# Retention and ELU feed-forward in one kernel: earlier weight loads, two-bank turns and another order of the matrix work

## The chip, the cores and the metric

The kernel runs on one core of a Trainium2 chip. The metric is the device time of one execution in microseconds (us). Before the change it was 322.56 us, the median of three runs (321.85 to 322.69). Lower is better.

## The reference, cut to what matters

```python
# q, k, v: (8, 8, 576, 64) float32; w_in (512, 2048), w_out (2048, 512)
scores = (1 / sqrt(64)) * q @ k.transpose(0, 1, 3, 2)
gamma  = 1 - 2 ** (-5 - arange(8))
Dmat   = where(rel >= 0, gamma ** rel, 0)        # rel = query position - key position
attn   = (scores * Dmat) @ v
x      = attn.transpose(0, 2, 1, 3).reshape(4608, 512)
h      = x @ w_in                                # "FFN1"
g      = where(h > 0, h, exp(min(h, 0)) - 1)     # ELU
out    = g @ w_out                               # "FFN2"
```

The kernel cuts the 4608 rows into 36 units of 128 rows. A unit goes through these steps: load q, k, v; cast to bf16; turn q and k (a transpose); scores; mask; products with v and with a running state; x. FFN1 and FFN2 work on groups of one to four units. Units 0 to 11 are turned by TensorE, units 12 to 35 by a DMA transpose.

## The kernel before

These are the parts that the change and the argument touch. Cuts are marked with `...`. The pools `ps_s`, `ps_h`, `ps_o` and so on lie in PSUM, the memory that TensorE writes its results to; a tile is a named buffer in a pool. A bank is a part of PSUM. A slot is one piece of FFN1 or FFN2 work in the order that the kernel builds. V, A and G are copies on VectorE, ScalarE and GpSimd. The w_in weights come in four pieces, one for each call of `load_w_in`.

```python
def turn(u, bank=None):
    t = tpool.tile([P, 2, HP, P], BF16, ...)
    n = kns[u]
    if u < PE_TURNED:                                  # 12
        pool, tag = bank or (ps_s, "sc")
        ps = pool.tile([P, 2, HP, P], BF16, name="tr", tag=tag)      # one tile for both halves
        for c in range(2):
            for hp in range(HP):
                nc.tensor.transpose(ps[:, c, hp], n[:, c, hp * P : (hp + 1) * P], ident)
        nc.vector.tensor_copy(t[:, 0], ps[:, 0])
        nc.scalar.copy(t[:, 1], ps[:, 1])
    else:
        nc.sync.dma_start_transpose(...)
    qkTs[u] = t

def finish(n=0):                                       # the ELU's last step, some slots late
    while late and late[0][0] <= slot[0] - n:
        _, gt_, ph, m, _ = late.pop(0)
        nc.vector.scalar_tensor_tensor(gt_, ph, 0.0, m, ALU.max, ALU.min)

# the start: units 0 to 2, then FFN1 of group 0
for u in range(3):
    scores(u); inter(u); state(u); masks(u)
    if u == 1:
        G(seen, raws[2][0][0:1, 0, 0, 0:1])            # GpSimd waits for unit 2's q ...
        load_w_in(0)                                   # ... and only then issues w_in
    if u < 2:
        cast(u + 1, A, G); scale_v(u + 1); dummy(3); turn(u + 1, h)
    else:
        for n in range(1, 4): load_w_in(n)
        load_w_out(0, 0, 8); load_w_out(0, 8, 16)
        dummy(6)                                       # warm-up matmuls, result not used
    intra(u); put_x(u); state_out(u); dummy(2)
...
for n in range(16):
    f1(0, n, m if n % 4 == 3 else None)
    if n == 3: turn(3)
    if n == 5:
        scale_v(3)
        load_w_out(1, 0, 16)                           # issued by GpSimd in mid-FFN1
    if n == 7: scores(3); masks(3)                     # one 128x1024 instruction
    if n == 11: product(3)
...
# steady part: FFN1 slots of group g merged with FFN2 slots of group g-1
while a < len(f1s) or b < len(f2s):
    if b * len(f1s) < a * len(f2s) and b < len(f2s) or a >= len(f1s):
        slots.append(f2s[b]); b += 1
    else:
        slots.append(f1s[a]); a += 1
```

## Time and profile before

| what | value | where it is read |
|---|---|---|
| span of the profiled execution | 320.8 us | first line of the page |
| TensorE (PE) busy | 305.0 us, 95% | busy table |
| VectorE, ScalarE, GpSimd busy | 58%, 43%, 45% | busy table |
| first FFN1 matmul | 19.99 us | timeline of PE |
| first FFN2 matmul | 37.76 us | timeline of PE |
| wait for an ELU result | 1.50 us at 27.8 us | timeline of PE |
| PE idle, 56 to 72 us | 2.20 us | windows |

Three lines of the page follow: busy us and share of the span for each engine; the busy tenths of PE in 40 slices; and the share of the DMA engines.

```profile
PE 305.0 (95%) x2961; PEld 173.4 (54%) x2998; DVE 185.9 (58%) x295; ACT 137.3 (43%) x255; POOL 143.5 (45%) x224
...
PE   7878999899999999999999999999999999999995
...
DMA  9999999997999999999898969777225200000021
```

Nothing but PE is near its limit over the whole span, so only PE's idle time can be won. The DMA engines are busy for most of the first 200 us (6 to 9 tenths in each of the first 25 slices).

The timeline of PE at the start (start us, duration, engine, line, operation, output and inputs, count, and in brackets the idle time before it and what ended it; `ph` is FFN1's result, `tr` a turn, `sc` the scores):

```profile
19.99 2.77 PE L322 MATMUL ph<-xt,w_in_sb 128*128 128x384 bf16 x16 [1.48 <-DMA w_in_sb<-in_moe_w_in_dram]
22.60 0.61 PE L190 MATMUL tr<-ident,qkn 128*128 128x128 bf16 x8
23.31 2.77 PE L322 MATMUL ph<-xt,w_in_sb 128*128 128x384 bf16 x16
26.01 0.42 PE L206 MATMUL sc<-qkT 64*64 64x128 bf16 x16
26.36 1.47 PE L322 MATMUL ph<-xt,w_in_sb 128*128 128x384 bf16 x8
29.34 1.46 PE L322 MATMUL ph<-xt,w_in_sb 128*128 128x384 bf16 x8 [1.50 <-DVE g L306]
```

PE waits 1.48 us for the first piece of w_in and later 1.50 us for VectorE's ELU result. GpSimd's timeline shows what held that result:

```profile
25.93 1.04 POOL L177 TENSOR_TENSOR vn<-rv,gk 128x512 bf16<-128x512 f32 x1
26.92 1.22 POOL L100 DMA_DIRECT2D w_out_sb<-in_moe_w_out_dram  x1
28.17 1.94 POOL L329 TENSOR_SCALAR m<-e 128x384 bf16<-128x384 f32 x4
```

The four `m` steps of the ELU stand behind the 1.22 us issue of a weight load.

Later, around unit 6, the chain of waits shows PE with nothing to run (start us, duration, what):

```profile
58.61 0.44 DVE qkT L191
...
59.07 0.59 ACT qkT L192
...
59.71 0.45 PE sc L206 x16
...
60.18 1.23 DVE pt L215
61.40 0.61 DVE xt L279
...
62.05 1.00 PE ph L322 x15
```

The turn's two copies run one after the other, and then mask and x separate the scores from the next FFN1. Both kinds of PE waits (first the copies, then x) stand in PE's timeline as 0.24 us and 1.23 us:

```profile
59.71 0.42 PE L206 MATMUL sc<-qkT 64*64 64x128 bf16 x16 [0.24 <-ACT qkT L192]
...
62.05 1.05 PE L322 MATMUL ph<-xt,w_in_sb 128*128 128x128 bf16 x16 [1.23 <-DVE xt L279]
```

The next lines are from the table of waits of ScalarE and from the windows view (stretch; length; PE busy and matmuls; PEld busy and weight loads; DVE; ACT; POOL; granted clock; DMA share; GB/s; the granted clock is the share of full TensorE speed that the profile records):

```profile
ACT qkT L192 <- DVE qkT L191: 9.4, 10, 2.5
```

```profile
56.00:72.00 16.00, 13.80 (x282) 11.38 (x277) 11.24 (x16) 8.52 (x17) 10.50 (x15) 1.00 1.02 212
...
104.00:180.00 76.00, 74.54 (x737) 39.76 (x748) 53.76 (x83) 34.17 (x67) 38.25 (x59) 1.00 1.02 191
180.00:300.00 120.00, 119.26 (x923) 57.14 (x936) 68.22 (x95) 50.11 (x88) 47.97 (x72) 1.00 0.44 96
```

### The profile page before, as it was taken

The page shows a single profiled execution, that of the slowest core. Times are in us where ns is not written, and L with a number is a line of the kernel's source. Part 1 is how long each engine was busy: PE and PEld are TensorE (multiplying, and loading weights), DVE is VectorE, ACT ScalarE, POOL GpSimd, SP SyncE. Part 2 cuts the span into 40 slices and gives each one's busy share as a digit, 9 for nine tenths or more (in the row PEclk, how much of TensorE's full clock was granted, in tenths as well). Part 3 has the DMA queues.
Part 4 walks back from the last instruction along what each step waited for, and adds up shares of the span by engine and source line. Part 5 has one row for each costly group of instructions (what it writes and reads, how often), then busy time and mean ns, then how long its engine had stood idle before and what let it go on. Part 6 is the DMA issues. An engine that isn't in the chain of part 4 may idle for free.

```text
span 320.8 us, 7515 instructions
## 1 busy us (share of the span) xinstructions
PE 305.0 (95%) x2961; PEld 173.4 (54%) x2998; DVE 185.9 (58%) x295; ACT 137.3 (43%) x255; POOL 143.5 (45%) x224
## 2 busy tenths in 40 slices
PE   7878999899999999999999999999999999999995
PEld 3544888776766555555444444444444444444444
DVE  3656713766668677676676666666666655433400
ACT  6335513545543445444444444344444444434411
POOL 2867530755644555454444444444444433333300
PEclk9999999999999999999999999999999999999999
DMA  9999999997999999999898969777225200000021
GB/s 169 216 213 200 175 232 255 212 206 180 222 163 221 237 194 182 187 227 168 165 218 166 181 134 219 163 167 166 67 65 68 65 35 35 33 33 33 36 98 65
DMA packets 150195, 48.72 MB, mean 152 GB/s; under 512 B 138640, under 2 KB 146192, under 8 KB 150160
## 3 DMA queue, kind: packets, MB, share of 16 engines
q1 hardware_dynamic: 141888, 41.76, 65.4%
q0 software_dynamic: 6256, 4.19, 8.8%
q10 hardware_dynamic: 2016, 2.29, 2.6%
q8 instruction: 23, 0.38, 0.5%
q14 instruction: 12, 0.10, 0.1%
HBM read 36.70 MB, written 9.44 MB: 144 GB/s over the span
## 4 chain that ended last, share of the span: by engine, by line
PE 85%; DMA 4%; DVE 4%; issue 2%; SPq 2%; POOL 1%; ACT 1%; POOLq 0%
PE ph L322 37%; PE pm L347 32%; PE pmh L363 6%; PE sc L206 4%; DMA w_in_sb<-in_moe_w_in_dram 3%; PE o L266 2%; PE st L249 2%; PE o L232 2%; SPq L86 2%; DMA rqk<-in_q_dram 2%; DVE pt L215 1%; PE tr L190 1%; POOL m L329 1%; DVE xt L279 1%; ACT qkT L192 1%
## 5 line engine op out<-in xcount | busy, mean ns | idle before, releaser
L329 POOL TENSOR_SCALAR m<-e 128x512 bf16<-128x512 f32 (+1 forms) x156 | 92.2, 592 | 147.2 <-ACT e L327 139.8
L322 PE MATMUL ph<-xt,w_in_sb 128*128 128x512 bf16 (+3 forms) x820 | 144.9, 313 | 5.4 <-DVE g L306 1.7
L306 DVE SCALAR_TENSOR_TENSOR g<-ph,m 128x512 bf16<-128x512 f32 (+1 forms) x156 | 99.9, 647 | 81.7 <-POOL m L329 80.4
L327 ACT ACTIVATE e<-ph 128x512 f32<-128x512 f32 (+1 forms) x156 | 88.0, 564 | 123.0 <-PE ph L322 119.1
L347 PE MATMUL pm<-w_out_sb,g 128*128 128x512 bf16 x474 | 121.4, 379 | 2.3 <-issue 1.6
L322 PEld LDWEIGHTS <-w_in_sb 128*128 128x128 bf16 x832 | 71.9, 98 | 60.9 <-issue 3.6
L347 PEld LDWEIGHTS <-g 128*128 128x128 bf16 x496 | 47.2, 98 | 52.7 <-issue 0.5
L215 DVE TENSOR_TENSOR pt<-sc,mask 128x1024 bf16<-128x1024 f32 x36 | 44.0, 1222 | 14.4 <-PE sc L206 14.4
L177 POOL TENSOR_TENSOR vn<-rv,gk 128x512 bf16<-128x512 f32 x36 | 37.8, 1052 | 2.5 <-DMA rv<-in_v_dram 1.5
L279 DVE TENSOR_TENSOR xt<-o,gx 128x512 bf16<-128x512 f32 x36 | 24.5, 681 | 3.4 <-PE o L266 3.4
L354 ACT COPY ot<-pm 128x512 f32<-128x512 f32 x31 | 18.1, 585 | 16.7 <-PE pm L347 16.5
L258 ACT CAST sb<-st 128x256 bf16<-128x256 f32 x32 | 11.9, 373 | 18.1 <-PE st L249 15.3
L363 PE MATMUL pmh<-w_out_sb,g 128*128 128x256 bf16 x160 | 18.5, 273 | 0.5 <-ACT oth L375 0.5
L206 PEld LDWEIGHTS <-qkT 64*64 64x64 bf16 x576 | 9.2, 106 | 15.4 <-issue 9.1
L206 PE MATMUL sc<-qkT 64*64 64x128 bf16 x576 | 15.0, 222 | 2.2 <-ACT qkT L192 2.2
L363 PEld LDWEIGHTS <-g 128*128 128x128 bf16 x160 | 15.4, 98 | 2.8 <-issue 0.6
L168 DVE CAST qkn<-rqk 128x1024 bf16<-128x1024 f32 x24 | 16.4, 683 | 0.0
L266 PE MATMUL o<-pt,vn 128*64 128x128 bf16 x288 | 14.4, 221 | 0.0
L232 PE MATMUL o<-qkT,sb 64*64 64x128 bf16 (+1 forms) x256 | 12.3, 214 | 0.0
L384 PE MATMUL dum<-warm 128*128 128x512 bf16 x35 | 10.9, 431 | 1.4 <-DVE warm L108 1.3
L192 ACT COPY qkT<-tr 128x512 bf16<-128x512 bf16 x12 | 7.0, 583 | 9.5 <-DVE qkT L191 9.4
L249 PE MATMUL st<-vn,qkn 128*64 128x64 bf16 (+1 forms) x256 | 10.5, 200 | 0.6 <-POOL vn L177 0.6
(43 smaller groups left out, 82.0 us busy)
## 6 DMA issues: line engine op xcount, KB each, us to landing
rqk<-in_q_dram SPq DMA_DIRECT2D x32, 256.0 KB, 3.9
rqk<-in_k_dram SPq DMA_DIRECT2D x32, 256.0 KB, 4.3
rv<-in_v_dram SPq DMA_DIRECT2D x32, 256.0 KB, 4.6
out_dram<-ot SPq DMA_DIRECT2D x27, 256.0 KB, 2.3
w_in_sb<-in_moe_w_in_dram POOLq DMA_DIRECT2D x4, 512.0 KB, 9.5
out_dram<-oth ACTq DMA_DIRECT2D x9, 128.0 KB, 3.3
w_out_sb<-in_moe_w_out_dram POOLq DMA_DIRECT2D x2, 512.0 KB, 15.2
w_out_sb<-in_moe_w_out_dram POOLq DMA_DIRECT2D x1, 1024.0 KB, 12.7
```

The costliest lines, as they stand in the source:

```text
L177: nc.gpsimd.tensor_tensor(n, rv, gk[:, u % R].unsqueeze(2).to_broadcast([P, H, D]), ALU.mult)
L206: nc.tensor.matmul(sc[j * 64 : (j + 1) * 64, i, hp], t[r, 1, hp, j * 64 : (j + 1) * 64], t[r, 0, hp], start=(hp == 0), stop=(hp == HP - 1) ...
L215: nc.vector.tensor_tensor(pt.rearrange("p i h t -> p (i h) t"), scs[u].rearrange("p i h t -> p (i h) t"), m.unsqueeze(1).to_broadcast([P, ...
L232: nc.tensor.matmul(o[rows, hp, :n], sbs[u][rows, hp], qkTs[u][rows, 0, hp, :n], start=(hp == 0), stop=False, skip_group_check=True,)
L266: nc.tensor.matmul(o[i * D : (i + 1) * D, hp], vns[u][:, h], pts[u][:, i, hp], start=(u % R == 0 and hp == 0), stop=(hp == HP - 1), skip_g ...
L279: nc.vector.tensor_tensor(xts[g][:, :, i * P : (i + 1) * P], os_[u], gx[:, :, s0 : s0 + P], ALU.mult)
L306: nc.vector.scalar_tensor_tensor(gt_, ph, 0.0, m, ALU.max, ALU.min)
L322: nc.tensor.matmul(ph[:, i * n : (i + 1) * n], w_in_sb[:, j, f : f + P], xts[g][:, j, :n], start=(j == 0), stop=(j == KJ - 1), skip_group_ ...
L327: nc.scalar.activation(e[:, w], ph[:, w], AF.Exp)
L329: nc.gpsimd.tensor_scalar(m[:, w], e[:, w], -1.0, 1.0, ALU.add, ALU.mult)
L347: nc.tensor.matmul(pm, gts[g, ft][:, it * P : (it + 1) * P], w_out_sb[:, ft], start=(ft == 0), stop=(ft == NFT - 1))
L363: nc.tensor.matmul(pm, gts[g, ft][:, it * P : (it + 1) * P], w_out_sb[:, ft, c * 256 : c * 256 + 256], start=(ft == 0), stop=(ft == NFT - 1),)
```

## The change

Its intent is to take away waits of PE: bring w_in sooner; let VectorE and ScalarE copy a turn's halves at the same time from two banks; shorten what stands in front of ELU results; keep an FFN2 slot between a unit's scores and the FFN1 that needs its x; and shorten the end. The diff, cut to its core:

```diff
     def turn(u, bank=None):
-            ps = pool.tile([P, 2, HP, P], BF16, name="tr", tag=tag)
+            if bank:                                   # units 0 to 2
+                ps = [pool.tile([P, HP, P], BF16, name="tr", tag=tag) for c in range(2)]
+            else:                                      # units 3 to 11
+                both = ps_s.tile([P, 2, 2, HP, P], BF16, name="tr", tag="sc")
+                ps = [both[:, c, 0] for c in range(2)]
...
     def ffn2(g, s):
-        if late and (g, part * 4 + 3) >= late[0][4]:
-            finish()
+        while late and (g, part * 4 + 3) >= late[0][4]:
+            finish(slot[0] - late[0][0])               # no more than is needed
...
-        if u == 1:
-            G(seen, raws[2][0][0:1, 0, 0, 0:1])
-            load_w_in(0)
         if u < 2:
             cast(u + 1, A, G)
+            if u == 0:
+                load_w_in(0)
...
             load_w_out(0, 8, 16)
-            dummy(6)
+            load_w_out(1, 0, 16)
+            dummy(3)
...
             scale_v(3)
-            load_w_out(1, 0, 16)
         if n == 7:
             scores(3)
-            masks(3)
+            masks(3, 0)
+        if n == 8:
+            masks(3, 1)
+        if n == 9:                                     # before: after f1(1, 0)
+            load(4, nc.vector)
+            for u in range(5, 12): load(u)
...
-    ffn2_half(0, 1, m)
+    ffn2_half(0, 1, h)
     turn(4); ffn2_half(1, 1, h); scores(4); masks(4)
-    ffn2_half(2, 1, h); product(4); prep(5, A, G)
-    ffn2_half(3, 1, h); turn(5); f1(2, 0); scores(5); masks(5); prep(6, A, G)
-    f1(2, 1); f1(2, 2); turn(6); f1(2, 3)
+    prep(5, A, G); ffn2_half(2, 1, h); product(4)
+    turn(5); ffn2_half(3, 1, m); scores(5); masks(5); prep(6, A, G)
+    f1(2, 0); f1(2, 1); turn(6); f1(2, 2)              # f1(2, 3) becomes the first slot
...
-            if b * len(f1s) < a * len(f2s) and b < len(f2s) or a >= len(f1s):
+            if b * len(f1s) <= a * len(f2s) and b < len(f2s) or a >= len(f1s):
...
-            due[u] = due[last] + (start[g] - 1.6 - due[last]) * (u - last) / (u1 - last)
+            due[u] = due[last] + (start[g] - 1.0 - due[last]) * (u - last) / (u1 - last)
+        if PE_TURNED <= u + 3 < NU:                    # DMA transposes
+            events.append((at(0.4) if u + 2 < PE_TURNED else due[u], -1, u + 3))
...
-    for c in range(2):
-        ffn2_half(NU - 1, c, ((ps_s, "sc"), h)[c])
+    ffn2_cols(u, 0, 256, (ps_s, "sc"), V, nc.scalar)
+    ffn2_cols(u, 256, 384, h, A, nc.scalar)
+    ffn2_cols(u, 384, 512, (ps_st, "st"), V, nc.sync)
```

More of the change, by code (lines that the diff above doesn't have):

```diff
@@ L185, in turn @@
         if u < PE_TURNED:
-            pool, tag = bank or (ps_s, "sc")
-            ps = pool.tile([P, 2, HP, P], BF16, name="tr", tag=tag)
+            if bank:
+                pool, tag = bank
+                ps = [pool.tile([P, HP, P], BF16, name="tr", tag=tag) for c in range(2)]
+            else:
+                both = ps_s.tile([P, 2, 2, HP, P], BF16, name="tr", tag="sc")
+                ps = [both[:, c, 0] for c in range(2)]
             for c in range(2):
                 for hp in range(HP):
-                    nc.tensor.transpose(ps[:, c, hp], n[:, c, hp * P : (hp + 1) * P], ident)
-            nc.vector.tensor_copy(t[:, 0], ps[:, 0])
-            nc.scalar.copy(t[:, 1], ps[:, 1])
+                    nc.tensor.transpose(ps[c][:, hp], n[:, c, hp * P : (hp + 1) * P], ident)
+            nc.vector.tensor_copy(t[:, 0], ps[0])
+            nc.scalar.copy(t[:, 1], ps[1])
         else:
@@ L210, in scores, with masks @@
         scs[u] = sc
-    def masks(u):
-        pt = ppool.tile([P, 2, HP, P], BF16, name="pt", tag="pt")
+    def masks(u, i=None):
+        if u not in pts:
+            pts[u] = ppool.tile([P, 2, HP, P], BF16, name="pt", tag="pt")
         m = mask[:, 1 if u % R == 4 else 0]
+        s = slice(0, 2) if i is None else slice(i, i + 1)
         nc.vector.tensor_tensor(
-            pt.rearrange("p i h t -> p (i h) t"), scs[u].rearrange("p i h t -> p (i h) t"),
-            m.unsqueeze(1).to_broadcast([P, 2 * HP, P]), ALU.mult,
+            pts[u][:, s].rearrange("p i h t -> p (i h) t"), scs[u][:, s].rearrange("p i h t -> p (i h) t"),
+            m.unsqueeze(1).to_broadcast([P, (s.stop - s.start) * HP, P]), ALU.mult,
         )
-        pts[u] = pt
     def inter(u):
@@ L355, in ffn2, with ffn2_cols, ffn2_half @@
             (nc.scalar if i0 < 8 * P else nc.sync).dma_start(out[i0 : i0 + P, :], ot)
-    def ffn2_half(u, c, bank):
+    def ffn2_cols(u, c0, c1, bank, copy, queue):
         g, it = group_of[u]
         pool, tag = bank
-        pm = pool.tile([P, 256], FP32, name="pmh", tag=tag)
+        pm = pool.tile([P, c1 - c0], FP32, name="pmh", tag=tag)
         for ft in range(NFT):
             nc.tensor.matmul(
-                pm, gts[g, ft][:, it * P : (it + 1) * P], w_out_sb[:, ft, c * 256 : c * 256 + 256],
+                pm, gts[g, ft][:, it * P : (it + 1) * P], w_out_sb[:, ft, c0:c1],
                 start=(ft == 0), stop=(ft == NFT - 1),
             )
-        ot = opool.tile([P, 256], FP32, name="oth", tag="ot")
-        rows = out[u * P : (u + 1) * P, c * 256 : c * 256 + 256]
-        if u == NU - 1 and c == 1:
-            nc.scalar.copy(ot[:, :128], pm[:, :128])
-            nc.scalar.dma_start(rows[:, :128], ot[:, :128])
-            nc.vector.tensor_copy(ot[:, 128:], pm[:, 128:])
-            nc.sync.dma_start(rows[:, 128:], ot[:, 128:])
-        else:
-            (nc.scalar.copy if u % 2 else nc.vector.tensor_copy)(ot, pm)
-            nc.scalar.dma_start(rows, ot)
+        ot = opool.tile([P, c1 - c0], FP32, name="oth", tag="ot")
+        copy(ot, pm)
+        queue.dma_start(out[u * P : (u + 1) * P, c0:c1], ot)
+    def ffn2_half(u, c, bank):
+        ffn2_cols(u, c * 256, c * 256 + 256, bank, A if u % 2 else V, nc.scalar)
     V, A, G = nc.vector.tensor_copy, nc.scalar.copy, nc.gpsimd.tensor_copy
@@ L390, in prep @@
             scale_v(u)
-            if u >= PE_TURNED:
-                turn(u)
     nload = [12]
@@ L408 @@
     h, m = (ps_h, "ph"), (ps_m, "pm")
-    seen = const.tile([1, 1], FP32, name="seen")
     dummy(18)
@@ L453 @@
             scale_v(3)
-            load_w_out(1, 0, 16)
         if n == 7:
             scores(3)
-            masks(3)
+            masks(3, 0)
[3 more added lines that the diff above has]
+            load(4, nc.vector)
+            for u in range(5, 12):
+                load(u)
         if n == 11:
@@ L461 @@
         f1(1, n, m if n == 3 else None)
-        if n == 0:
-            load(4, nc.vector)
-            for u in range(5, 12):
-                load(u)
     finish()
@@ L474 @@
     masks(4)
+    prep(5, A, G)
     ffn2_half(2, 1, h)
     product(4)
-    prep(5, A, G)
-    ffn2_half(3, 1, h)
     turn(5)
-    f1(2, 0)
+    ffn2_half(3, 1, m)
     scores(5)
@@ L483 @@
     prep(6, A, G)
+    f1(2, 0)
     f1(2, 1)
+    turn(6)
     f1(2, 2)
-    turn(6)
-    f1(2, 3)
-    slots, start, now = [], {}, 0.0
+    slots, start, now = [(f1, 2, 3, 1.0)], {}, 1.0
     for g in range(3, NG + 1):
+        f1s, f2s = [], [(ffn2, g - 1, s, 1.0) for s in range(4 * len(GROUPS[g - 1]))]
+        if g < NG:
+            per = 4 // len(GROUPS[g])
+            f1s = [(f1, g, s, per * len(GROUPS[g]) / 4) for s in range(NFT // per)]
+        else:
+            f2s = f2s[:-4]
+        a, b = 0, 2 if g == 4 else 0
+        slots += f2s[:b]
+        now += b
         start[g] = now
-        f1s = [(f1, g, s, k * len(GROUPS[g]) * P / 512) for k in [4 // len(GROUPS[g])] for s in range(NFT // k)] if g < NG else []
-        n2 = len(GROUPS[g - 1]) - (g == NG)
-        f2s = [(ffn2, g - 1, s, 1.0) for s in range(4 * n2)]
-        a = b = 0
         while a < len(f1s) or b < len(f2s):
-            if b * len(f1s) < a * len(f2s) and b < len(f2s) or a >= len(f1s):
+            if b * len(f1s) <= a * len(f2s) and b < len(f2s) or a >= len(f1s):
                 slots.append(f2s[b])
@@ L513, with at @@
     for u in range(5, NU):
+        def at(share):
+            return due[u] + share * (due[u + 1] - due[u])
         events.append((due[u], 0, u))
         if u + 2 < PE_TURNED:
-            events.append(((due[u] + due[u + 1]) / 2, 1, u + 2))
+            events += [(due[u], -1, u + 2), (at(0.5), 1, u + 2)]
+        if PE_TURNED <= u + 3 < NU:
+            events.append((at(0.4) if u + 2 < PE_TURNED else due[u], -1, u + 3))
     events.sort()
@@ L522 @@
             _, kind, u = events.pop(0)
-            if kind == 1:
-                turn(u)
-                continue
-            if u + 2 < PE_TURNED:
-                prep(u + 2, A, G)
-            if u + 3 >= PE_TURNED:
-                prep(u + 3, V)
-            load_next()
-            stretch(u)
+            if kind == -1:
+                prep(u, *((A, G) if u < PE_TURNED else (V,)))
+                if u >= PE_TURNED:
+                    turn(u)
+            elif kind == 1:
+                turn(u)
+            else:
+                load_next()
+                stretch(u)
         f(g, s)
         now += d
-    for c in range(2):
-        ffn2_half(NU - 1, c, ((ps_s, "sc"), h)[c])
+    u = NU - 1
+    ffn2_cols(u, 0, 256, (ps_s, "sc"), V, nc.scalar)
+    ffn2_cols(u, 256, 384, h, A, nc.scalar)
+    ffn2_cols(u, 384, 512, (ps_st, "st"), V, nc.sync)
 _INS = ['q', 'k', 'v', 'moe_w_in', 'moe_w_out']
```

## The prediction

> **What bounds the kernel.** TensorE: 305.0 us busy of a 320.8 us span (busy table), granted clock 1.00 in every slice. The change removes no matrix work but three warm-up matmuls, so it can only shorten TensorE's 15.8 us of idle. By the windows table that idle lies: about 3.2 us before 16 us, 1.5 in 18–20, 1.5 in 28–30, 0.5 at 45, 0.5 in 54–60, 1.7 in 60–72, 1.0 in 72–104, 1.3 up to 180, 0.7 from 180 to 300, 3.7 at the end.
>
> **Step by step.**
>
> 1. *w_in one step sooner.* Before, its first DMA is issued at 11.58 us, behind a gate on unit 2's q, and lands 8.37 us later (chain of waits); the first FFN1 matmul starts at 19.99 after 1.5 us idle. After, it should issue near 10 us, and two-bank turns and fewer dummies bring unit 2's x earlier, so FFN1 should start near 18.5. I expect almost none of this to be kept: the DMA engines are saturated (DMA share above 1.2, 205–218 GB/s), the w_in pieces follow each other about 2.7 us apart, and weight loads already wait for the second piece at 23.30. Same bytes, same rate: it lands near 23 again. Gain 0.2 us.[...]
>
> 2. *Unit 3's mask in halves, w_out's second half issued earlier.* The 1.50 us gap at 27.8–29.3 waits for an ELU result (VectorE g), itself held by the w_out issue on GpSimd (1.22 in the timeline) and the 1.23 us mask on VectorE. The issue moves into GpSimd's idle time before 21 us; the mask becomes two pieces of about 0.65. Gain 1.3 us.
>
> 3. *Column halves.* Unit 0's second half no longer reuses the bank of unit 3's first: 0.46 us at 45.
>
> 4. *Turns through two banks, more work behind them.* Now ScalarE's copy waits for VectorE's (9.4 us, 10 times); in parallel the turn loses 0.43 us. With the new order FFN work covers the rest: the waits of 0.24–0.27 before scores of units 5 to 8 and 1.23 before group 3's FFN1 (scores, mask 1.22, xt 0.61, nothing else to run) should go. Gain 2.1 us in 54–72.
>
> 5. *FFN2 slot first in each merge*, one-at-a-time finishing: a further filler between a unit's scores and the FFN1 that needs its x. Of 2.3 us idle in 72–180, I take 1.1.
>
> 6. *Last columns in two banks.* VectorE's last copy no longer follows ScalarE's: 0.3 us.
>
> Sum 5.5 us. **Against it:** loads of units 4–11 start near 28 us instead of 35.5 and compete with w_out, whose pieces land near 31.4, 34.2 and 39.6 (issue plus time to landing). [...]the first is needed near 36, the last near 43, so the stall is 0 to 1 us. I deduct 0.3.
>
> **Prediction: 317.4 us** (−1.6%), 8 in 10 within 315.0 to 319.8. Faster by over 2%: 0.23; within 2%: 0.76; slower: 0.01.
>
> **What would show it.** First FFN1 matmul near 18.5, then a wait for w_in of over 1 us near 21.5–23; no gap near 28; TensorE idle below 0.8 us in the stretch that was 54–72; ScalarE's qkT copy no longer waiting for VectorE's; idle from 180 on unchanged.
>
> **What would make it wrong.** If the second w_in piece also lands earlier (unit 3's loads yielding), step 1 gains up to 1.5 us more. If the early unit loads starve w_out, TensorE stalls at the first column halves by 1–3 us. If the later x (due 1.0 slot ahead instead of 1.6) makes FFN1 wait, step 5 turns into a loss.

0.2, 1.3, 0.46, 2.1, 1.1 and 0.3 make 5.5 us, less 0.3 for the early loads 5.2, and 322.56 less 5.2 is 317.4.

## More of the kernel before

A caution for later: the trace has 2961 matmul records for 2998 weight loads, and the built program has 2998 of each. Some matmul records are missing, and a missing record looks like idle time (run 9).

## The result

| | before | changed | ratio of the fast runs, 95% interval |
|---|---|---|---|
| first measurement | 322.31 us (4 runs) | 319.00 us (4 runs, 318.29 to 319.70) | 0.9898, 0.9870 to 0.9925 |
| again, as a control | 322.49 us (11 runs) | 318.47 us (4 runs, 317.87 to 319.25) | 0.9879, 0.9864 to 0.9895 |

The times are medians. All outputs are right. A ratio is the mean time of one kernel's fast runs over that of the other's of the same rounds, so it is not quite the ratio of the medians. The change wins 3.3 us in the first measurement and 3.9 us in the second, by ratio times the median of before. That is inside the predicted range (315.0 to 319.8) and within 2%.

The busy line and the start of PE's timeline after the change:

```profile
PE 307.1 (97%) x2974; PEld 174.2 (55%) x3011; DVE 187.4 (59%) x297; ACT 136.9 (43%) x254; POOL 144.9 (46%) x223
```

```profile
17.56 2.76 PE L329 MATMUL ph<-xt,w_in_sb 128*128 128x384 bf16 x16 [0.24 <-DVE xt L286]
20.15 0.61 PE L195 MATMUL tr<-ident,qkn 128*128 128x128 bf16 x8
23.02 4.46 PE L329 MATMUL ph<-xt,w_in_sb 128*128 128x384 bf16 x16 [2.26 <-DMA w_in_sb<-in_moe_w_in_dram]
27.41 0.42 PE L211 MATMUL sc<-qkT 64*64 64x128 bf16 x16
27.76 2.14 PE L329 MATMUL ph<-xt,w_in_sb 128*128 128x384 bf16 x12
30.15 0.81 PE L329 MATMUL ph<-xt,w_in_sb 128*128 128x384 bf16 x4 [0.25 <-DVE rqk L83]
```

The gap of 1.50 us near 28 is gone. FFN1 starts 2.43 us sooner, then waits 2.26 us for the second piece of w_in, so that the matmuls behind it start at 23.02 (before: 23.31). The sixteen matmuls after it take 4.46 us instead of 2.77. The windows view tells why (the figure after POOL's is the granted clock):

```profile
22.00:24.00 2.00, 0.98 (x4) 0.51 (x5) 0.81 (x2) 0.50 (x1) 0.00 (x0) 0.82 1.24 206
24.00:26.00 2.00, 2.00 (x7) 0.91 (x6) 0.49 (x1) 0.82 (x2) 0.51 (x1) 0.50 1.25 205
26.00:28.00 2.00, 2.00 (x25) 1.06 (x24) 0.74 (x3) 1.07 (x3) 1.76 (x3) 0.83 1.43 201
```

The granted clock is halved here (0.50). Reading the clock in half-microsecond windows, 0.77 in 23.0 to 23.5 and 0.82 in 26.5 to 27.0 with 0.50 between them, the drop lasts from about 23.27 to 26.68 us, worked out from these shares. In this execution, 0.7 us longer than the median one, FFN2 starts at 37.92 us, no sooner than before (37.76): the whole gain of the start is gone. In the control's profiled execution there is a shorter wait (1.76 us), a clock of 1.00 in each window from 16 to 32 us, and FFN2 starts at 36.41.

The waits of PE and of ScalarE after the change, then the same windows as before:

```profile
PE ph L329 <- DMA w_in_sb<-in_moe_w_in_dram: 2.3, 1, 2.3
...
PE ph L329 <- DVE xt L286: 0.5, 2, 0.3
PE sc L211 <- ACT qkT L197: 0.5, 2, 0.2
```

```profile
ACT qkT L197 <- DVE qkT L196: 5.9, 9, 1.2
ACT qkT L197 <- PE tr L195: 3.6, 3, 1.7
```

```profile
56.00:72.00 16.00, 15.50 (x270) 11.87 (x271) 10.75 (x16) 9.01 (x18) 9.26 (x14) 1.00 0.90 203
...
104.00:180.00 76.00, 75.22 (x738) 39.69 (x748) 54.66 (x82) 34.24 (x67) 38.43 (x60) 1.00 1.08 194
180.00:300.00 120.00, 119.27 (x923) 57.06 (x936) 67.85 (x94) 49.51 (x87) 48.23 (x72) 1.00 0.41 92
```

Idle time in 56 to 72 us fell from 2.20 to 0.50 us. But ScalarE's copy still waits for VectorE's in nine of twelve turns. In only the first three turns, which use two separate tiles, does it wait for TensorE instead (3.6 us). Those of units 3 to 11 use one tile, laid out to span two banks, and by the waits (5.9 us) ScalarE's copy there still stands behind VectorE's. (In the built program nine of the twelve copies wait on VectorE's semaphore and three on TensorE's.) For most turns, what was called "two banks" did not happen.

At the end, PE's last matmul to the last output issue took 0.65 us before (317.33 to 317.98) and 0.41 us after (314.73 to 315.14).

### The profile page after: what moved, and what is told of

Read it like the earlier page. It is cut to its first block, busy times and chain, and to the rows that moved or that the text cites. A ratio compares the mean times of both kernels' runs of the same rounds, so it can differ in the third digit from the quotient of the medians.

```text
span 318.0 us, 7546 instructions
## 1 busy us (share of the span) xinstructions
PE 307.1 (97%) x2974; PEld 174.2 (55%) x3011; DVE 187.4 (59%) x297; ACT 136.9 (43%) x254; POOL 144.9 (46%) x223
## 3 DMA queue, kind: packets, MB, share of 16 engines
q0 software_dynamic: 6256, 4.19, 8.8%
q10 hardware_dynamic: 2016, 2.29, 2.2%
## 4 chain that ended last, share of the span: by engine, by line
PE 82%; DMA 6%; issue 3%; POOL 3%; SPq 2%; DVE 2%; ACT 0%; POOLq 0%; DVEq 0%
PE ph L329 35%; PE pm L354 31%; PE pmh L370 6%; PE sc L211 3%; DMA w_in_sb<-in_moe_w_in_dram 3%; PE o L273 2%; SPq L86 2%; PE st L256 2%; PE o L239 2%; DMA rv<-in_v_dram 2%; DMA qkT<-qkn 1%; POOL m L336 1%; POOL vn L177 1%; DVE pt L223 1%; PE tr L195 1%
## 5 line engine op out<-in xcount | busy, mean ns | idle before, releaser
L336 POOL TENSOR_SCALAR m<-e 128x512 bf16<-128x512 f32 (+1 forms) x156 | 93.7, 601 | 142.0 <-ACT e L334 137.1
L329 PE MATMUL ph<-xt,w_in_sb 128*128 128x512 bf16 (+3 forms) x816 | 146.5, 315 | 3.9 <-DMA w_in_sb<-in_moe_w_in_dram 2.3
L354 PE MATMUL pm<-w_out_sb,g 128*128 128x512 bf16 x478 | 122.8, 379 | 1.5 <-issue 0.8
L354 PEld LDWEIGHTS <-g 128*128 128x128 bf16 x496 | 47.8, 98 | 53.2 <-issue 0.2
L223 DVE TENSOR_TENSOR pt<-sc,mask 128x1024 bf16<-128x1024 f32 (+1 forms) x37 | 44.2, 1194 | 14.6 <-PE sc L211 14.4
L370 PE MATMUL pmh<-w_out_sb,g 128*128 128x256 bf16 (+1 forms) x176 | 18.3, 263 | 0.0
L370 PEld LDWEIGHTS <-g 128*128 128x128 bf16 x176 | 15.7, 98 | 1.9
L375 DVE COPY oth<-pmh 128x256 f32<-128x256 f32 (+1 forms) x6 | 2.4, 400 | 18.0 <-PE pmh L370 18.0
```

The lines of the kernel that those rows point to most:

```text
L223: nc.vector.tensor_tensor(pts[u][:, s].rearrange("p i h t -> p (i h) t"), scs[u][:, s].rearrange("p i h t -> p (i h) t"), m.unsqueeze(1).t ...
L329: nc.tensor.matmul(ph[:, i * n : (i + 1) * n], w_in_sb[:, j, f : f + P], xts[g][:, j, :n], start=(j == 0), stop=(j == KJ - 1), skip_group_ ...
L336: nc.gpsimd.tensor_scalar(m[:, w], e[:, w], -1.0, 1.0, ALU.add, ALU.mult)
L354: nc.tensor.matmul(pm, gts[g, ft][:, it * P : (it + 1) * P], w_out_sb[:, ft], start=(ft == 0), stop=(ft == NFT - 1))
L370: nc.tensor.matmul(pm, gts[g, ft][:, it * P : (it + 1) * P], w_out_sb[:, ft, c0:c1], start=(ft == 0), stop=(ft == NFT - 1),)
```

## The experiments

Twelve kernels were run. The runs of one call share a chip and their runs of the kernel before, so they are compared with each other directly; across calls only through the ratio to before.

### 1. Fill the wait for w_in

```diff
         if n == 3:
             turn(3)
+            fill = ps_o.tile([P, 512], FP32, name="fill", tag="o")
+            for _ in range(10):
+                nc.tensor.matmul(fill, warm[:, :P], warm, start=True, stop=True)
```

> The changed kernel with ten more warm-up matmuls (into unit 3's still unused o bank) behind unit 3's turn, where TensorE waited 2.26 us for the second w_in piece. Theory (the head is paced by w_in's arrival, and the long wait costs a second time by halving the granted clock afterwards): clock 1.00 in every slice, the sixteen FFN1 matmuls after the wait take 2.8 us instead of 4.46, first FFN2 column half near 36.3 instead of 37.9, 317.3 to 318.3 us. Rival (the clock drop is a matter of the profiled execution alone and the other executions don't have it): same as the changed kernel, 319.0 within 0.4.

Measured: 320.08 us median (319.38 to 321.64, six runs), ratio 0.9930 (0.9908 to 0.9953). The clock was 1.00 in all six runs and the sixteen matmuls took 2.76 us, as the theory says; but only two of the changed kernel's eight executions had shown the drop (mean clock 0.993), so six without it are no proof that the filler removed it. FFN2 started at 36.83 instead of 37.92. But the time did not follow; the expected 317.3 to 318.3 was missed by about 2 us, and by its ratio this kernel is even 1.0 to 1.6 us slower than the changed one (0.9898 and 0.9879). Of the 1.09 us won at FFN2, 0.54 was left at unit 4's scores (48.40 against 48.94), and 0.21 at unit 35's (263.22 against 263.43). On the way PE waited for ScalarE's cast of unit 4 (0.37 us) and for the DMA transpose of unit 12 (0.5 us). So in this one trace what is won at the start is partly given back where PE waits for what the DMA engines bring. Why three of its executions took over 320 us at full clock stays open.

### 2. The old gate of w_in, in the changed kernel

```diff
+        if u == 1:
+            G(seen, raws[2][0][0:1, 0, 0, 0:1])
+            load_w_in(0)
         if u < 2:
             cast(u + 1, A, G)
-            if u == 0:
-                load_w_in(0)
```

> The changed kernel with the old gate and the old place of the first w_in load put back. Theory (w_in one step sooner only moves the wait from before the first FFN1 matmul to before the fifth group): FFN1 starts near 19.5 to 20, the later wait is below 0.5 us, the second w_in piece lands near 23 as in both kernels, no slice at half clock, time equal to the changed kernel or up to 0.8 us below it. Rival (the early issue is worth its 2 us): 320 to 321 us.

Measured: 320.07 us median of six, ratio of the fast runs 0.9912 (0.9893 to 0.9931), which overlaps the changed kernel's. The profiled execution was a slow one (323.72), so its time is not used. Its start agrees with the theory on where the wait is: it waits 2.21 us before the first FFN1 matmul (19.63), and the second piece is there at 23.01, as in both kernels. The theory expected full clock, and two of the five fast runs and the slow one had a mean clock of 0.995. In the slow one, the only one with a trace, the lost clock does not belong to this wait: the sixteen matmuls behind it took 2.77 us, as in the trace of before. Behind a wait of 3.33 us for unit 12's DMA transpose the matmuls took longer than elsewhere in this trace: 0.64 us instead of 0.42 for the scores at 97.39, 1.38 instead of 0.81 for three FFN2 matmuls at 99.57. The FFN1 matmuls at 100.79 took their usual time (1.04).

```profile
19.63 2.77 PE L329 MATMUL ph<-xt,w_in_sb 128*128 128x384 bf16 x16 [2.21 <-DMA w_in_sb<-in_moe_w_in_dram]
...
97.39 0.64 PE L211 MATMUL sc<-qkT 64*64 64x128 bf16 x16 [3.33 <-DMA qkT<-qkn]
```

Why 2.21 us cost no clock here and 2.26 us did in the changed kernel's first trace was not shown. Side by side: the granted clock was lower, or the matmuls were slower, behind waits of 2.26 us (changed kernel, clock 0.50), 2.84 us (run 11), 3.33 us (here) and 4.03 us (run 4, clock 0.53 and then 0.50). They were not behind waits of 1.76 us (control, clock 1.00), 2.21 us (here) and 2.29 us (run 7, clock 1.00). So the length of the wait alone does not sort these traces; no run was made to find what does.

### 3. Only the early w_in, in the kernel before

```diff
-        if u == 1:
-            G(seen, raws[2][0][0:1, 0, 0, 0:1])
-            load_w_in(0)
         if u < 2:
             cast(u + 1, A, G)
+            if u == 0:
+                load_w_in(0)
```

> The kernel before with the first w_in load one step sooner and its gate removed, nothing else. Theory: first FFN1 matmul 0.5 to 1.5 us sooner, but second piece again near 23 us, so 322.3 within 0.6, perhaps a little slower where the wait halves the clock. Rival: faster by over 1 us.

Measured: ratio 1.0055 (1.0022 to 1.0088), a loss of 1.8 us. In the profiled fast run FFN1 starts at 19.41, 0.58 us sooner, then waits until 23.89. Unit 2's v now comes late, too: GpSimd waits 1.97 us for it. Three of the five fast runs had a clock of 0.995; where in them is not recorded. Alone, this step is a loss.

### 4. Load unit 3 behind the weights

```diff
-    for u in range(4):
+    for u in range(3):
         load(u)
...
             for n in range(1, 4):
                 load_w_in(n)
+            load(3, nc.gpsimd)          # and unit 3's steps three to four tiles later,
...                                      # units 4 to 11 loaded after f1(1, 0)
```

> The changed kernel with unit 3's q, k and v loaded only after the w_in loads are issued (their 0.79 MB stood ahead of w_in in the saturated DMA engines), unit 3's steps three to four FFN1 tiles later, and the loads of units 4 to 11 held until group 1's FFN1. Theory (bytes ahead of w_in set the pace): the second w_in piece lands 2 to 3.5 us sooner (19.5 to 21), no wait for it above 0.5 us, no half clock, first FFN2 column half near 34 to 35, 315.5 to 317.0 us. If w_in's pace is set by its own queue and not by the bytes beside it: second piece still near 23, 318.5 to 319.5 us.

Measured: ratio 1.0258 (1.0222 to 1.0294), slower by 8 us. PE waited 4.03 and 3.48 us for the casts of unit 3's q and k, and the clock was 0.53 in 28 to 30 us and 0.50 in each window from 30 to 38 us; the sixteen matmuls at 38.78 still took 4.21 us instead of 2.76. One half of the theory held: the second w_in piece was there before 21.18 us, where FFN1 went on after a wait for something else. But unit 3's own load was starved. Its three DMAs of 256 KB were issued from 17.14 us on, and GpSimd got the v only at 36.61:

```profile
36.61 1.04 POOL L177 TENSOR_TENSOR vn<-rv,gk 128x512 bf16<-128x512 f32 x1 [12.14 <-DMA rv<-in_v_dram]
```

So 0.79 MB took 19.5 us, 40 GB/s, in stretches where all DMA together moved 182 to 204 GB/s. The two queues did not get equal shares of the bytes: beside the weights of the GpSimd queue, the unit loads got about a fifth (40 of 190 GB/s, the mean of 18 to 38 us). In the first 60 us of before, the profile counts 29103 packets for 7.33 MB on the queue of the loads (252 B each) and 6256 for 4.19 MB on that of the weights (670 B each). By an estimate with these sizes, the 0.79 MB of loads are about 3100 packets and the other 3.0 MB of those 20 us (190 GB/s) about 4500, so the packets were shared more evenly than the bytes. Two things in the changed kernel fit this. Its loads of units 4 to 11, issued from 30.15 us instead of 35.49, brought unit 4's k no sooner (GpSimd's cast at 43.71 against 42.50). And these loads did not starve w_out either: PE ran 80 column-half matmuls from 37.92 without a stop.

### 5. Control

The changed kernel again, without an edit.

> The changed kernel itself, as the control on the chip of the three runs beside it: ratio 0.990 within 0.003 to the kernel before, some executions with a granted clock of 0.993 to 0.995 (half clock after the wait for the second w_in piece).

Measured: 318.47 us, ratio 0.9879 (0.9864 to 0.9895). One of the four runs had a clock of 0.993, as one of the first four had. The control itself was expected at 0.990 within 0.003, and was.

### 6. Unit 12's transpose ahead of one unit's loads

```diff
-            events.append((at(0.4) if u + 2 < PE_TURNED else due[u], -1, u + 3))
+            events.append((due[u], -1, u + 3))
```

> The changed kernel with the transpose of unit 12 put on the SyncE queue ahead of one unit's q, k and v loads, where the kernel before has it. Theory (the change pushed this transpose behind 0.79 MB of loads; it is issued 4.75 us later than before, lands at 94.82 and TensorE's scores of unit 12 wait for it, the wait varying from 0.3 to 3.3 us between executions): no wait for a DMA transpose at unit 12, 0.3 to 0.8 us below the control on the mean, smaller spread. Rival (unit 12 is not what binds): same as the control within 0.2 us.

Measured: 318.94 us (318.82 to 319.44, four runs), ratio 0.9891 (0.9877 to 0.9906), not better than the control. The wait at unit 12 is gone from the trace, so the place on the queue decides it, but in the mean it costs nothing that these runs can show. The spread was narrow here (0.6 us) and not in run 12, which has the same edit, so nothing is claimed about spread.

This trace shows a trade at the start. The second w_in piece came a microsecond sooner than in the changed kernel's first trace, though nothing in the edit touches the start: executions differ by this much. And unit 3's v came so late that the gap of before was back:

```profile
21.97 2.77 PE L329 MATMUL ph<-xt,w_in_sb 128*128 128x384 bf16 x16 [0.90 <-DMA w_in_sb<-in_moe_w_in_dram]
...
28.26 0.81 PE L329 MATMUL ph<-xt,w_in_sb 128*128 128x384 bf16 x4 [1.41 <-DVE g L313]
```

```profile
26.09 1.04 POOL L177 TENSOR_TENSOR vn<-rv,gk 128x512 bf16<-128x512 f32 x1 [1.47 <-DMA rv<-in_v_dram]
```

Here, with a DMA share of 1.2 and more (windows of 18 to 30 us), w_in came earlier and v later. It is no fixed exchange: in run 10 the second piece came early, too (22.27), and PE waited only 0.26 us for the ELU result at 27.05.

### 7. The same with the old gate

Edits of runs 2 and 6 together.

> As the run before it, and with the old gate and place of the first w_in load. Theory: neither the wait of over 2 us with half clock after it nor the wait at unit 12 is left, 317.5 to 318.8 us, all executions at a clock of 1.00, at or below the control by 0.5 to 1.5 us. Rival (the early w_in is worth something once unit 12 is repaired): slower than the run before it by over 0.5 us.

Measured: 319.95 us, ratio 0.9923 (0.9910 to 0.9935), slower than run 6 by 1.0 us by the medians. The profiled one waits 2.29 us in front of FFN1 and keeps the full clock (1.00 in every window up to 300 us). Three of its five runs had a clock of 0.995; they left no trace, so where they lost it is not known. My theory fell: in the changed kernel the early issue is worth about 1 us against the gate (in run 2, without run 6's edit, 0.5 to 1.1 us, within the noise). The changed start with its three fewer dummy matmuls is ready for FFN1 at about 17.5 us, and the gate then leaves a long wait. The two full-clock runs of this kernel (319.42 and 319.55) are 0.5 and 0.6 us above run 6's median. So about half of what the early issue is worth here looks like avoided loss of clock (the three runs at 0.995 took 319.95 to 320.32); this last step is argued from two runs and not shown.

### 8. Only the issue of w_out's second half, in the kernel before

```diff
             load_w_out(0, 8, 16)
+            load_w_out(1, 0, 16)
...
             scale_v(3)
-            load_w_out(1, 0, 16)
```

> The kernel before with only the issue of w_out's second half moved from unit 3's middle to the other weight loads. Theory: the 1.50 us gap at 27.8 to 29.3 us shrinks to 0.3 to 0.8 (the unsplit mask of 1.23 us is left in front of the ELU result) and the head ends 0.7 to 1.2 us sooner: ratio 0.997 to 0.9965. If the mask is the whole cause of the gap: 1.50 us gap still there, ratio 1.000.

Measured: 321.09 us, ratio 0.9959 (0.9947 to 0.9971), a gain of 1.3 us. The gap of 1.50 us is down to 0.43, with the mask still in one piece:

```profile
27.54 1.46 PE L322 MATMUL ph<-xt,w_in_sb 128*128 128x384 bf16 x8 [0.43 <-DVE g L306]
```

FFN2 started at 35.96 us, sooner than in any profiled execution of the changed kernel. Of these 1.80 us against before, 0.71 is not the edit's: in this execution the FFN1 behind the second w_in piece happened to start at 22.60 instead of 23.31. The time, over six runs, gives the edit 1.3 us, as much as was predicted for the whole step. In the control, with the mask in halves, two waits of 0.26 and 0.25 us are left at the same place (the second for VectorE's one-element write that starts unit 4's load), so the halves add nothing that can be seen.

### 9. Only the order, in the kernel before

Everything from the column halves on as in the changed kernel (unit 0's second half in another bank, the sequence up to group 2, FFN2 first in each merge, `finish` one at a time, the new due times). w_in, w_out, mask, unit loads, turns and last columns stay as before.

> The kernel before with only the order changed: the sequence from the column halves on (other bank for unit 0's second half, more FFN work behind each turn), FFN2 first in each merge, one-at-a-time finishing. The w_in and w_out issues, the mask, the unit loads, the turns through one bank and the last columns are as before. Theory (order, not the two banks, removes the waits of 54 to 72 us; in the changed kernel's trace ScalarE's copy still waits for VectorE's in nine of twelve turns): 2.0 to 2.8 us below before, ratio 0.9915 to 0.994. Rival (the two-bank turn carries that gain): less than 1.2 us, ratio above 0.996.

Measured: 319.59 us, ratio 0.9922 (0.9906 to 0.9939), a gain of 2.5 us. ScalarE's copy waits for VectorE's in all twelve turns (9.6 us), and PE is idle for 0.45 us in 56 to 72 us all the same, against 2.20 before. The order takes away the waits, not the banks.

This trace also settles another question. It happens to have nearly all its matmul records:

```profile
104.00:180.00 76.00, 75.90 (x751) 39.79 (x750) 54.58 (x83) 33.80 (x67) 38.91 (x60) 1.00 1.09 191
180.00:300.00 120.00, 120.00 (x938) 57.04 (x937) 67.87 (x95) 49.52 (x87) 47.97 (x71) 1.00 0.42 93
```

From 180 to 300 us PE is busy without a break. In the traces of before and after there are 13 matmuls fewer than weight loads in that stretch, and 0.74 and 0.73 us of "idle". The 1.46 us that I had read as idle in 104 to 180 us of before stands beside 11 fewer matmuls than weight loads. It is, nearly all of it, missing records: seven of its gaps are 0.16 us in front of three FFN2 matmuls where the program has four, and run 10, with the merge order of before and 749 matmuls beside 747 loads, has 0.10 us idle there. The profiled execution was the slowest of the six (320.94, the others 319.32 to 319.80), and it shows what the late place of unit 12's transpose can cost in one execution:

```profile
95.89 0.42 PE L207 MATMUL sc<-qkT 64*64 64x128 bf16 x16 [1.50 <-DMA qkT<-qkn]
```

### 10. FFN1 first in each merge again, in the changed kernel

```diff
-        a, b = 0, 2 if g == 4 else 0
+        a, b = 0, 0
-            if b * len(f1s) <= a * len(f2s) ...
+            if b * len(f1s) < a * len(f2s) ...
-            due[u] = due[last] + (start[g] - 1.0 - due[last]) * ...
+            due[u] = due[last] + (start[g] - 1.6 - due[last]) * ...
```

> The changed kernel with the FFN1 slot first in each merge again and the units due 1.6 slots ahead, as before. Theory: the first FFN1 of groups 3 and following stands directly behind the scores of the next unit and waits for x again (about 1 us at group 3, a few tenths at later groups): 0.7 to 1.5 us above the changed kernel, ratio 0.990 to 0.9925. Rival (part of the idle that this step was to remove is matmul records missing from the trace, not idle): within 0.4 us of the changed kernel, ratio 0.987 to 0.989.

Measured: 319.68 us, ratio 0.9927 (0.9910 to 0.9943). Against the changed kernel's two ratios that is a loss of 0.9 to 1.5 us. PE is idle for 1.35 us in 56 to 72 us again, 0.83 of it in front of group 3's first FFN1:

```profile
59.54 1.05 PE L329 MATMUL ph<-xt,w_in_sb 128*128 128x128 bf16 x16 [0.83 <-DVE g L313]
```

So FFN2 first is worth about 1 us, but at group 3, near 60 us, and not spread over 72 to 180 us. By the profile the wait there is for VectorE's ELU result and not for x, as the theory had it.

### 11. Really two banks

```diff
-                both = ps_s.tile([P, 2, 2, HP, P], BF16, name="tr", tag="sc")
-                ps = [both[:, c, 0] for c in range(2)]
+                ps = [ps_s.tile([P, HP, P], BF16, name="tr", tag=f"sc{c}") for c in range(2)]
...
-        sc = ps_s.tile([P, 2, HP, P], FP32, name="sc", tag="sc")
+        sc = [ps_s.tile([P, HP, P], FP32, name="sc", tag=f"sc{i}") for i in range(2)]
```

> The changed kernel with the score tile made of two one-bank tiles, so that every turn of units 3 to 11 really has two tiles; the mask is two instructions in every unit. Theory: ScalarE's qkT copy waits for TensorE and no longer for VectorE in all turns (its 5.9 us of waiting for VectorE go), but TensorE waited only 0.5 us for these copies in the changed kernel, so the time moves by at most 0.5 us either way, ratio 0.986 to 0.990. If the serial copies bind behind other work: 1 us or more faster.

Measured: 318.77 us median, ratio 0.9895 (0.9874 to 0.9917), the same as the changed kernel. ScalarE's wait for VectorE is nearly gone:

```profile
ACT qkT L196 <- PE tr L194: 4.2, 3, 1.8
ACT qkT L196 <- DVE qkT L195: 1.1, 1, 1.1
```

The wait was between two readers of one tile (5.9 us in the changed kernel, 1.1 us here), and taking it away wins no time (the edit also cuts every mask in two, so a small gain could be hidden by that). PE waited 0.5 us for these copies in the changed kernel and 0.2 us here. The profiled execution was this kernel's worst (322.47, clock 0.989). In it PE waited 2.84 us for an ELU result behind unit 3's late v, the same trade as in run 6, and the clock was lower afterwards: 0.84 as the mean of 16 to 38 us, and the eight matmuls behind the wait took 2.72 us instead of 1.48.

### 12. A candidate

Six dummies in the wait for w_in (as run 1) and unit 12's transpose ahead (as run 6), in the changed kernel.

> Candidate: the changed kernel with six warm-up matmuls in the wait for the second w_in piece and unit 12's transpose ahead of one unit's loads. Theory: no slice at half clock, no wait at unit 12, 317.3 to 318.3 us, narrow spread, ratio 0.984 to 0.988. Rival (neither wait costs anything in a usual execution): ratio 0.988 to 0.990, no better than the changed kernel.

Measured: 318.95 us median (318.47 to 321.65), ratio 0.9913 (0.9886 to 0.9941), no better than the changed kernel. It is a miss: in its trace the wait for w_in is down to 0.62 us and the one at unit 12 is gone, and the time is no shorter. No version beats the changed kernel.

## Why the prediction was right, and where it was not

The time (319.0 and 318.5 us against 317.4, range 315.0 to 319.8) and the class were right. The gain was 3.3 to 3.9 us instead of 5.2 (322.56 to 317.4). That the time fell into the range is partly luck: the prediction put the banks and the order into one term, so that it came out though only the order worked, and the terms that were too high had room in a range of 4.8 us.

| step | predicted gain, us | what the runs show |
|---|---|---|
| 1 w_in sooner | 0.2 | alone a loss of 1.8; against the gate, in the changed start, 0.5 to 1.1 |
| 2 w_out issue, mask halves | 1.3 | 1.3, from the w_out issue alone |
| 3 other bank for a column half | 0.46 | the wait is gone; part of run 9 |
| 4 turns in two banks, more work behind them | 2.1 | 1.7 in 56 to 72 us (1.9 in the predicted 54 to 72: 2.44 to 0.50 idle), from the order, not from the banks |
| 5 FFN2 first | 1.1 in 72 to 180 us | 0.9 to 1.5, but at group 3; most of it is contained in the 1.7 of step 4 |
| 6 last columns | 0.3 | 0.24 by the timeline; not run alone |
| contention of early unit loads | -0.3 | no stall of PE at w_out; not run alone |

Runs 8 and 9 together account for the change. Multiplied, 0.9959 and 0.9922 give 0.9881, beside 0.9898 and 0.9879 for the whole. With the intervals of the two (0.0012 and 0.0017 each way) all the rest together is zero within about 0.7 us, by an estimate from these numbers.

**Step 1 was right about the waits and wrong about the worth.** It said that FFN1 would start near 18.5 us (17.56), then wait for over 1 us (2.26), and that the second piece would come near 23 again (23.02). The argument was that full DMA engines deliver the same bytes by the same time, the author's estimate. The traces do not settle it: the FFN1 behind the second piece started between 21.97 and 23.89 us in the executions with the early issue that waited for it, and between 22.60 and 23.31 in those with the gate; and run 4, with unit 3's loads out of the way, had the piece before 21.18, so what is asked first does matter. Two things were missing from it. The wait of 2.26 us was followed by a granted clock of 0.50. And where w_in was asked for early, GpSimd waited for unit 2's or unit 3's v in some traces (1.97 us in run 3, 1.47 in run 6, 2.86 in run 11).

**Step 2 was right in size and half right in cause.** The gap was laid to two things; moving one of them gave the predicted 1.3 us.

**Step 4 was right in place and wrong in mechanism.** The text expected "ScalarE's qkT copy no longer waiting for VectorE's". It still waited in nine of twelve turns, and run 11 shows that this did not matter. In the trace of before, with one tile for both halves, ScalarE's copies wait 9.4 us in all for VectorE's. The changed kernel's turns wait too (5.9 us), with the halves laid out in two banks of one tile; so these traces cannot tell a wait for the bank from a wait for the tile. Here two banks inside one tile, as laid out, were not enough; separate tiles were (1.1 us in run 11). No run tries two engines on one bank.

**Step 5 is the term that was mis-sized.** "Of 2.3 us idle in 72–180, I take 1.1": most of those 2.3 us were missing matmul records (nearly all of the 1.46 in 104 to 180 us, and two gaps of 0.16 before that). What the step really does, the filler at group 3, had mostly been counted already in step 4. For steps 3, 4 and 5 together 3.66 us were predicted, and run 9 measured 2.5. The difference, 1.16 us, is about the size of step 5's term (1.1), and it is most of the distance between 5.2 and the measured gain. The forecast "idle from 180 on unchanged" held, but only because there was no real idle time there.

The prediction did not see one new wait: the change puts unit 12's transpose behind one unit's loads, and PE then waited for it between 0.36 us (control) and 3.33 us (run 2) where a wait is recorded. Run 6 shows no cost of it in the mean.

What stays open: why some executions of these kernels take 1 to 2 us more at full clock (run 1; unit 12's wait is a candidate, but run 12 without it still has a run of 320.11); what the mask halves, the last columns and the early loads are worth alone.

## What to carry to other kernels

Before counting idle time of TensorE as something to win, compare the number of matmul records with the number of weight loads in the same window; here a gap of 0.16 us beside three matmuls where the program has four was a lost record. When one load is moved forward while the DMA engines are busy, look for what else is waiting for bytes: here unit 2's or unit 3's v came late in some traces with the early w_in (GpSimd waited 1.97, 1.47 and 2.86 us in runs 3, 6 and 11). Look at the granted clock behind long waits, too: it was 0.50 behind one of 2.26 us and 1.00 behind one of 2.29 us, and what decides it is not known from these runs. Instructions that only issue DMAs are worth moving out of an engine's path when that engine feeds the critical one: here that single line gave 1.3 us, a third of the gain.
